# A transposed read in two halves, and one gate product in each bundle of a fused convolution and channel mix

## The chip, the cores and the metric

The kernel runs on one core of a Trainium2 chip. The metric is the device time of one execution in microseconds; three runs of the kernel before took 412.99, 415.35 and 415.41, with a median of 415.35.

## The reference

Input x is 8 batches of 4160 tokens of 192 channels. The first part is a causal convolution along the tokens with 7 taps; the taps of each of the 8 heads (24 channels each) are the softmax of its row of weights. The second part is a channel mix on its output y:

```python
y_prev = shift(y)                        # one token back, zero at the start
xk = mu_k * y + (1 - mu_k) * y_prev      # = y_prev + mu_k * (y - y_prev)
xr = mu_r * y + (1 - mu_r) * y_prev
k  = relu(xk @ w_k) ** 2                 # 192 -> 1024
v  = k @ w_v                             # 1024 -> 192
out = sigmoid(xr @ w_r) * v              # 192 -> 192
```

## The kernel before

Batches are worked on in four pairs. The channel mix needs y with channels on the partitions (yT: 64 channels of each of the two batches), cut into **steps** of 512 tokens of both batches (step 4 is tokens 1792 to 2304 of the first pair, step 5 the 512 after it). A step has 8 K products of 1024 columns (ps_k), a relu of each on ScalarE (k_sb, L605), a square on VectorE (k, L619), and V in two **quads** of 256 tokens (ps_v, L681). VectorE also forms d = y - y_prev (`diff`, L536), then xk and xr by scaling d with mu and adding y (L567, L573). R is `r` (L642 to L657, ps_r), its sigmoid `r_out` (L661), and `v_out` (L694) multiplies V by it and stores the output through SyncE (L705). Products, convolutions and R all take PSUM buffers from one ring of four (L56).

The order of all instructions is written out by hand. Four K products make a **bundle**, about 6 us long; there are 65, numbered from 0. `bundle_rest` (L930) gives one bundle's order: squares and VectorE's mixing work, K products 0 to 2, one R (the first in the table `rq` for this bundle), the first half of a quad's V, K product 3, any further R, the convolution units due in this bundle, and the second half of V. Tables give what falls due in a bundle: `mix_a`, `mix_b`, `mix_c` are run at three places among the squares, `late` at the end; `rq` and `rs` hold R and its sigmoid. SyncE's instructions are transfers alone, and they are issued in the order of the program, each with its waits.

The convolution works on **groups** of tokens of a pair. The first groups of the first pair are convolved on TensorE straight into the transposed layout. Every later group is convolved with tokens on the partitions, cast by ScalarE into a tile y (L337; two buffers), written to a buffer in memory by SyncE (`y_write`, L458), and read back transposed into yT by a DMA (`y_read`, L484). Group 4 (tokens 1920 to 3040 of the first pair) is the first of this kind. Its writes are put in `late` of bundle 3, its read in `mix_c` of bundle 4; groups 5, 6 and 7 are dense too and have a read of their own each. From group 8 on the units are "sparse" (`conv_sparse`, L350): each takes two ring buffers and fills two y tiles, and those groups are already read in two halves. The units of group 8 fall in bundles 14 to 17, those of group 9 in bundles 22 to 25.

In a dense group, y holds blocks of 56 tokens: 64 partitions hold one row of blocks, the other 64 another, and `y_write` needs four transfers (i: first or second half of the tokens, j: which 64 partitions).

xk and xr have two buffers each. With two, the R of step s must be done before step s + 2 is mixed, so line L808 caps R's bundle. This cap matters only after the first pair's last step, which is half as long: bundle 14 has two R's, bundle 17 has none.

Of the kernel before, what the change touches and what calls it, by code (L numbers as in the profile page):

```python
# [8 lines left out]
BF16 = mybir.dt.bfloat16  # L9
# [5 lines left out]
def kernel(  # L15
# [17 lines left out]
    P = 128  # L33
    NF = DF // P
    Q = 64
    NC = D // Q
# [8 lines left out]
    STEP = 512  # L45
# [7 lines left out]
    two = ctx.enter_context(tc.tile_pool(name="two", bufs=2))  # L53
    three = ctx.enter_context(tc.tile_pool(name="three", bufs=3))
# [19 lines left out]
    T0, LAST = S - TAIL, len(steps) - 1  # L74
# [11 lines left out]
    first_bundle = [bundle_of[st[3]] for st in steps]  # L86
# [365 lines left out]
    def new_yT(p):  # L452
        yTs[p] = two.tile([P, 3, -(-(YC + S) // 16) * 16], BF16, tag="yT", name="yT")
        y_drams[p] = dram.tile([NROW, 2 * D], BF16, tag=f"y{p % 2}", name="y_dram")
        nc.vector.memset(yTs[p][:, :, 0:YC], 0.0)


    def y_write(g):  # L458
        p, base, nb, _, _ = groups[g]
        if base == 0:  # L460
            new_yT(p)
        if g in sparse:
            m = nb // 4
            for half in range(2):
                for j in range(4):
                    nc.sync.dma_start(
                        out=bass.AP(
                            tensor=y_drams[p].tensor,
                            offset=y_drams[p].offset + (base + (2 * half * nb + j) * TB) * 2 * D,
                            ap=[[2 * D, TB], [4 * TB * 2 * D, 2 * m], [1, 2 * D]],  # L470
                        ),
                        in_=ys[g][half][32 * j : 32 * j + TB, :, :],
                    )
            return
        m = nb // 2
        for j in range(2):
            for i in range(2):
                r0 = base + (i * nb + j * m) * HB
                nc.sync.dma_start(  # L479
                    out=y_drams[p][r0 : r0 + m * HB, :].rearrange("(n t) c -> t n c", t=HB),  # L480
                    in_=ys[g][j * Q : j * Q + HB, i * m : (i + 1) * m, :],
                )
# [33 lines left out]
    diffs, xks, xrs = {}, {}, {}  # L516
# [23 lines left out]
    def mix(s, i, sl=slice(0, NC)):  # L540

        L = steps[s][2]
        d = diffs[s]
        if s == 0 and i == 0:
            if sl.start == 0:
                xks[s] = two.tile([P, NC, STEP], BF16, tag="xk", name="xk")
            t = xks[s]
            c = sl.start
            nc.vector.scalar_tensor_tensor(
                out=t[:, c, :L],  # L550
                in0=d[:, c, :L],
                scalar=mu[:, i, c : c + 1],
                in1=y_of(s, sl, 0)[:, 0, :],
                op0=ALU.mult,
                op1=ALU.add,
            )
            return
        scale(s, i, *range(sl.start, sl.stop))
        add_y(s, i, sl)

    def scale(s, i, *cs):
        L = steps[s][2]
        if s not in (xks, xrs)[i]:
            (xks, xrs)[i][s] = two.tile([P, NC, STEP], BF16, tag=("xk", "xr")[i], name=("xk", "xr")[i])
        t = (xks, xrs)[i][s]
        for c in cs:
            nc.vector.tensor_scalar(  # L567
                out=t[:, c, :L], in0=diffs[s][:, c, :L], scalar1=mu[:, i, c : c + 1], scalar2=None, op0=ALU.mult
            )
# [163 lines left out]
    early, rq, rs, xt, mix_a, mix_b, mix_c, vq, late = ({} for _ in range(9))  # L733

    def at(table, b, fn, *a):
        table.setdefault(b, []).append((fn, a))
# [7 lines left out]
    for g, (p, base, nb, fb, on_pe) in enumerate(groups):  # L744
        if g < 3:
            continue
        if p == 0:
            xs = {3: [1, 1], 4: [2, 2, 3, 3], 5: [4, 4, 5, 5]}[g]
        elif g not in sparse:
            xs = [fb - 9] * 2 + [fb - 7] * 2  # L750
        else:
            xs = {8: [14, 15, 16, 17], 9: [22, 23, 24, 25]}.get(g, [fb - 13, fb - 11, fb - 9, fb - 7])
        for i, b in enumerate(xs):
            xt.setdefault(b, []).append((g, i))
        if not on_pe:
            at(late, xs[-1], y_write, g)
        if g in sparse:
            at(late, max(fb - 5, xs[-1] + 2), y_read, g, slice(0, 1), 2)
            at(late, fb - 2, y_read, g, slice(1, 2), 2)
            b, b1 = {8: (9, 12), 9: (17, 18), 10: (24, 25)}.get(g, (fb - 19, fb - 16))  # L760
            at(early, b, x_tile, g)
            at(early, b, load_x, g, (0,))
            b = b1
            at(early, b, tie_x, g, 1)
            at(early, b, load_x, g, (1,))
            continue
        if not on_pe:
            at(mix_c if g == 4 else late, xs[-1] + (1 if g < 6 else 2), y_read, g)
        if g > 4:

            b = {5: 1, 6: 3, 7: 7}.get(g)
            b = first_bundle[first_step[p]] + (-15, -11, -7, -3)[(g - 6) % 4] if b is None else b
            table = {5: mix_a, 7: mix_c}.get(g, early)
            at(table, b, x_tile, g)
            at(table, b, load_x, g)
    for s, (p, t0, L, n0, ns) in enumerate(steps):
        fb = first_bundle[s]
        if s == 0:
            at(mix_a, 1, mix, s, 1)
            continue  # L780
        if s == 1:
            at(mix_b, 1, scale, s, 1, 0, 1)
            at(late, 2, scale, s, 1, 2)
            at(late, 2, add_y, s, 1)
        else:
            if s == 2:
                at(mix_c, 1, diff, s)
            elif s == 4:
                at(mix_b, fb - 1, diff, s)
            else:  # L790
                at(mix_c, fb - 2, diff, s)
            at(mix_b if s == 4 else mix_a, fb - 1, scale, s, 0, 0)
            at(mix_b, fb - 1, scale, s, 0, 1, 2)
            at(mix_c, fb - 1, add_y, s, 0)
            if s == 2:
                at(mix_a, fb, scale, s, 1, 0)
                at(mix_b, fb, scale, s, 1, 1)
            else:
                at(mix_c, fb - 1, scale, s, 1, 0)
                at(mix_a, fb, scale, s, 1, 1)  # L800
            at(mix_b, fb, scale, s, 1, 2)
            at(mix_b, fb, add_y, s, 1)
        if s == LAST - 1 or s < LAST and steps[s + 1][0] > p:
            at(late, fb - 1, keep_tail, p)
    for s, j, vb in quads:
        b = vb - (s == LAST)
        if 0 < s < LAST - 1:
            b = min(b, first_bundle[s + 2] - 2 + j)  # L808
        at(rq, b, r, s, j)
        at(rs, b, r_out, s, j)  # L810
        if s == LAST:
            at(late, vb, v_last, s, j)
        else:
            vq.setdefault(vb, []).append((s, j))
# [249 lines left out]
```

## Time and profile before

| | |
|---|---|
| runs, us | 412.99, 415.35, 415.41 |
| profiled execution, us | 412.98 |
| its span, us | 411.3 |
| TensorE busy (PE) | 401.3 us, 98% |
| VectorE busy (DVE) | 371.1 us, 90% |
| ScalarE busy (ACT) | 354.6 us, 86% |
| granted clock of TensorE | 0.999 |
| transposed reads of y (L488) | 14 |
| idle of d (L536) for such a read | 0.8 us, once |

Times within the profile count from the start of the span. PE is TensorE's matmuls and PEld its weight loads, SPq is SyncE's queue of transfers. The name of a group of instructions gives line, operation, output and inputs; an arrow "<-" behind an idle time names what released the instruction. An entry of SPq covers the issue of a transfer, not its movement.

### The profile page before, as it was taken

The numbers are of one execution on the slowest core, as the hardware profiler recorded it, in microseconds if no ns is written. First come the engines' busy times: TensorE is split into PE (matmuls) and PEld (weight loads), VectorE is DVE, ScalarE is ACT, GpSimd is POOL, SyncE is SP. The second block draws the span as 40 slices with busy tenths as digits, with TensorE's granted clock in tenths as the row PEclk, the third lists the DMA queues.
The fourth block names the chain that finished last, engine by engine and source line by source line (L and its number), as shares of the span: only waits on it lengthen the run. The fifth ranks groups of instructions, "written<-read, shape, count | busy, mean of one in ns | idle before, by whom it ended". The sixth has DMA issues, their size and how long they took to land.

```text
span 411.3 us, 17419 instructions
## 1 busy us (share of the span) xinstructions
PE 401.3 (98%) x7670; PEld 302.5 (74%) x7670; DVE 371.1 (90%) x672; ACT 354.6 (86%) x426; POOL 57.8 (14%) x91
## 2 busy tenths in 40 slices
PE   7899999999999999999999999999999999999996
PEld 4667767777777777777777777777777778777795
DVE  5899799999899998989999999999999899999973
ACT  6799978889998889988898998889898878877781
POOL 8623023030042002204020022100000001000000
PEclk9999999999999999999999999999999999999999
DMA  8999989997769988989995997979523756221223
GB/s 141 191 202 187 196 202 181 247 187 172 161 105 229 238 181 143 218 228 165 174 190 148 215 186 140 173 178 194 141 78 86 199 145 158 79 73 46 80 78 116
DMA packets 139091, 66.35 MB, mean 161 GB/s; under 512 B 89332, under 2 KB 139016, under 8 KB 139016
## 3 DMA queue, kind: packets, MB, share of 16 engines
q1 hardware_dynamic: 95672, 48.32, 48.3%
q0 software_dynamic: 42544, 16.36, 34.5%
q8 instruction: 60, 0.98, 1.0%
q10 hardware_dynamic: 800, 0.57, 0.5%
q14 instruction: 15, 0.12, 0.1%
HBM read 33.29 MB, written 36.99 MB: 171 GB/s over the span
## 4 chain that ended last, share of the span: by engine, by line
PE 87%; DMA 4%; DVE 4%; ACT 2%; POOL 1%; issue 1%; SPq 0%; POOLq 0%; ACTq 0%
PE ps_v L681 39%; PE ps_k L593 37%; PE ps_r L650 7%; PE ps_c L364 2%; DMA yT<-y_dram 2%; DMA wk<-in_moe_w_k_dram 2%; DVE k L619 2%; PE ps_v L633 1%; ACT k_sb L605 1%; DMA y_dram<-y 1%; PE ps_c L319 1%; ACT y L337 0%; DVE d L536 0%; POOL xb L154 0%; SPq L479 0%
## 5 line engine op out<-in xcount | busy, mean ns | idle before, releaser
L605 ACT ACTIVATE k_sb<-ps_k 128x1024 bf16<-128x1024 f32 x260 | 253.3, 1040 | 35.9 <-PE ps_k L593 35.2
L619 DVE TENSOR_TENSOR k<-k_sb 128x1024 bf16<-128x1024 bf16 x260 | 173.8, 689 | 26.0 <-ACT k_sb L605 25.9
L593 PE MATMUL ps_k<-xk,wk 64*128 64x512 bf16 (+1 forms) x1632 | 191.6, 367 | 2.0 <-DMA wk<-in_moe_w_k_dram 1.6
L681 PE MATMUL ps_v<-wv,k 64*128 64x192 bf16 x4032 | 188.6, 243 | 0.2 <-DVE k L619 0.2
L681 PEld LDWEIGHTS <-k 64*128 64x128 bf16 x4032 | 168.4, 94 | 13.2 <-issue 4.8
L593 PEld LDWEIGHTS <-wk 64*128 64x128 bf16 x1632 | 83.8, 94 | 57.2 <-DMA wk<-in_moe_w_k_dram 1.8
L154 POOL DMA_DIRECT2D xb<-in_x_dram x62 | 44.1, 720 | 142.8 <-DVE xb L125 58.7
L697 DVE TENSOR_TENSOR o_sb<-ps_v,r_sb 128x768 f32<-128x768 f32 x64 | 60.9, 951 | 3.3 <-issue 2.4
L661 ACT ACTIVATE r_sb<-ps_r 128x768 bf16<-128x768 f32 x65 | 53.6, 826 | 8.7 <-PE ps_v L681 7.0
L337 ACT CAST y<-ps_c 128x960 bf16<-128x960 f32 (+2 forms) x84 | 52.8, 709 | 0.2 <-DMA y_dram<-y 0.2
L650 PEld LDWEIGHTS <-xr 64*128 64x128 bf16 x780 | 34.8, 94 | 14.9 <-issue 1.0
L650 PE MATMUL ps_r<-wr,xr 64*128 64x192 bf16 x780 | 43.2, 243 | 0.5 <-DVE o_sb L697 0.5
L567 DVE TENSOR_SCALAR xr<-d,mu 128x512 bf16<-128x512 bf16 (+1 forms) x102 | 35.6, 353 | 0.0
L536 DVE TENSOR_TENSOR d<-yT 128x1536 bf16<-128x1536 bf16 (+4 forms) x36 | 31.2, 867 | 1.9 <-ACT yT L423 1.0
L567 DVE TENSOR_SCALAR xk<-d,mu 128x512 bf16<-128x512 bf16 (+1 forms) x99 | 32.1, 354 | 0.1
L573 DVE TENSOR_TENSOR xr<-xr,yT 128x1536 bf16<-128x1536 bf16 (+1 forms) x33 | 31.1, 942 | 1.1
L573 DVE TENSOR_TENSOR xk<-xk,yT 128x1536 bf16<-128x1536 bf16 (+3 forms) x33 | 30.6, 927 | 0.1
L520 POOL COPY y_tail<-yT 128x195 bf16<-128x195 bf16 x4 | 3.0, 762 | 89.3 <-DMA yT<-y_dram 89.3
L364 PEld LDWEIGHTS <-toe 32*32 32x32 bf16 x640 | 4.3, 87 | 8.9 <-issue 7.7
L364 PE MATMUL ps_c<-xb,toe 32*32 32x240 bf16 x640 | 9.4, 267 | 0.4 <-ACT k_sb L605 0.4
L127 POOL MEMSET xb<- 32x384 bf16 x3 | 1.2, 408 | 56.1 <-DVE xb L125 49.8
L413 PEld LDWEIGHTS <-xb 128*32 128x32 bf16 (+3 forms) x264 | 4.4, 104 | 2.5 <-ACT xb L247 1.1
(58 smaller groups left out, 65.0 us busy)
## 6 DMA issues: line engine op xcount, KB each, us to landing
out_dram<-o_sb SPq DMA_DIRECT2D x128, 192.0 KB
xb<-in_x_dram POOLq DMA_DIRECT2D x52, 240.0 KB, 8.5
y_dram<-y SPq DMA_DIRECT2D x40, 195.0 KB
y_dram<-y SPq DMA_DIRECT2D x16, 210.0 KB
xb<-in_x_dram POOLq DMA_DIRECT2D x4, 228.0 KB, 4.6
xb<-in_x_dram POOLq DMA_DIRECT2D x4, 192.0 KB, 6.6
wk<-in_moe_w_k_dram POOLq DMA_DIRECT2D x4, 192.0 KB, 7.4
xb<-in_x_dram POOLq DMA_DIRECT2D x2, 216.0 KB, 4.7
```

The lines of the kernel that those rows point to most:

```text
L154: nc.gpsimd.dma_start(out=xb[q0 : q0 + rows, lo:hi, s, :], in_=bass.AP(tensor=x.tensor, offset=x.offset + (b * S + t0 + lo * step) * D, ap ...
L337: nc.scalar.copy(out=bass.AP(tensor=y.tensor, offset=y.offset + d, ap=[y.ap[0], [m * 2 * D, 2], [2 * D, m], [Q, 2], [1, b - a]],), in_=bas ...
L536: nc.vector.tensor_tensor(out=shaped(s, diffs[s][:, cs, :L]), in0=y_of(s, cs, 1), in1=y_of(s, cs, 0), op=ALU.subtract)
L567: nc.vector.tensor_scalar(out=t[:, c, :L], in0=diffs[s][:, c, :L], scalar1=mu[:, i, c : c + 1], scalar2=None, op0=ALU.mult)
L573: nc.vector.tensor_tensor(out=o, in0=o, in1=y_of(s, sl, 0), op=ALU.add)
L593: nc.tensor.matmul(out=ps[:, i, f * L : (f + 1) * L], lhsT=wk[r, c, fs], rhs=xk[r, c, :L], start=c == 0 and f == 0, stop=c == NC - 1 and f ...
L605: nc.scalar.activation(out=k_sb, in_=ps.rearrange("p a b -> p (a b)"), func=AF.Relu)
L619: nc.vector.tensor_tensor(out=o, in0=i, in1=i, op=ALU.mult)
L650: nc.tensor.matmul(out=ps[:, i, k * D : (k + 1) * D], lhsT=xr[q, c, ts], rhs=wr[q, c, :], start=c == 0, stop=c == NC - 1,)
L661: nc.scalar.activation(out=r_sbs[s, j], in_=r_ps.pop((s, j))[:, :, 0 : 2 * D], func=AF.Sigmoid)
L681: nc.tensor.matmul(out=v_ps[s, j][:, bank, k * D : (k + 1) * D], lhsT=k2s[s][q, f, t * P : (t + 1) * P], rhs=wv[q, f, :], start=half == 0 ...
L697: nc.vector.tensor_tensor(out=o_sb.rearrange("p (b t) d -> p b (t d)", b=2), in0=v_ps.pop((s, j)), in1=r_sbs.pop((s, j)), op=ALU.mult,)
```

## The change

There are three edits.

1. `y_write`'s loop over token halves becomes the outer one, so the two transfers of the first 560 tokens of a group of 1120 are issued first. This holds for all four dense groups.
2. Group 4's transposed read becomes two: its first 560 tokens in `mix_c` of bundle 4, the second 560 in `late` of bundle 4. The reads of groups 5 to 7 stay whole and where they were.
3. xr gets three buffers, and the cap on R's bundle goes. R is then in the bundle of its own V quad: one R in each of bundles 14 to 17, where there were 2, 1, 1 and 0. No other bundle's R moves.

```diff
         m = nb // 2
-        for j in range(2):
-            for i in range(2):
+        for i in range(2):
+            for j in range(2):
                 r0 = base + (i * nb + j * m) * HB
                 nc.sync.dma_start(
...
         if s not in (xks, xrs)[i]:
-            (xks, xrs)[i][s] = two.tile([P, NC, STEP], BF16, tag=("xk", "xr")[i], name=("xk", "xr")[i])
+            (xks, xrs)[i][s] = (two, three)[i].tile([P, NC, STEP], BF16, tag=("xk", "xr")[i], name=("xk", "xr")[i])
...
         if not on_pe:
-            at(mix_c if g == 4 else late, xs[-1] + (1 if g < 6 else 2), y_read, g)
+            if g == 4:
+                at(mix_c, 4, y_read, g, slice(0, 1), 2)
+                at(late, 4, y_read, g, slice(1, 2), 2)
+            else:
+                at(late, xs[-1] + (1 if g < 6 else 2), y_read, g)
...
     for s, j, vb in quads:
         b = vb - (s == LAST)
-        if 0 < s < LAST - 1:
-            b = min(b, first_bundle[s + 2] - 2 + j)
         at(rq, b, r, s, j)
         at(rs, b, r_out, s, j)
```

## The prediction

> **What bounds the kernel now.** I read the busy totals, then who waited for whom, then the chain that ended last around each wait of TensorE, then the stages.
>
> ```profile
> PE 401.3 (98%) x7670; PEld 302.5 (74%) x7670; DVE 371.1 (90%) x672; ACT 354.6 (86%) x426; POOL 57.8 (14%) x91
> ```
>
> TensorE is idle for 411.3 - 401.3 = 10.0 us, most of it in the first 20 us. So nothing that leaves its work alone can bring much: the question is which stalls after 20 us the two edits touch. The list of waits has two of them, each with the wait that stands behind it:
>
> ```profile
> DVE d L536 <- DMA yT<-y_dram: 0.8, 1, 0.8
> PE ps_r L650 <- DVE o_sb L697: 0.5, 1, 0.5
> PE ps_c L364 <- ACT k_sb L605: 0.4, 1, 0.4
> ACT y L337 <- DMA y_dram<-y: 0.2, 1, 0.2
> ```
>
> The chain, in order of time (start, length), ties the first two together: y's write, the transposed read, d, then VectorE's queue up to o_sb, whose PSUM buffer R's product then takes.
>
> ```profile
> 38.16 4.37 DMA y_dram<-y
> 42.68 7.31 DMA yT<-y_dram
> 50.01 0.98 DVE d L536
> 55.70 0.88 DVE o_sb L697
> 56.62 0.67 PE ps_r L650 x12
> ```
>
> SyncE's queue in the same stretch (start, length of the issue):
>
> ```profile
> 39.51 2.02 SPq L705 DMA_DIRECT2D out_dram<-o_sb  x2
> 42.68 3.93 SPq L488 DMA_TRANSPOSE yT<-y_dram  x1
> 46.72 1.82 SPq L705 DMA_DIRECT2D out_dram<-o_sb  x2
> ```
>
> I measure a bundle from the start of its predecessor's second run of 32 V matmuls to the start of its own. In the stages (from:to, length, then busy PE, PEld, DVE, ACT, POOL, clock, DMA share, GB/s) these are bundles 5 and 7, then 14 to 17, then 24:
>
> ```profile
> 40.36:46.72 6.36, 6.36 (x121) 4.58 (x118) 5.61 (x10) 6.26 (x9) 0.00 (x0) 1.00 0.73 181
> 52.46:59.73 7.27, 6.70 (x120) 4.54 (x116) 7.24 (x14) 5.34 (x7) 0.38 (x1) 1.00 0.74 192
> ...
> 96.05:103.40 7.35, 6.95 (x150) 5.04 (x146) 6.41 (x13) 7.25 (x10) 0.00 (x0) 1.00 0.50 137
> 103.40:109.61 6.21, 6.21 (x166) 5.58 (x158) 5.44 (x13) 5.83 (x8) 0.00 (x0) 1.00 0.80 149
> 109.61:116.08 6.47, 6.47 (x150) 4.58 (x134) 6.16 (x10) 6.47 (x10) 0.00 (x0) 1.00 0.62 157
> 116.08:121.77 5.69, 5.69 (x130) 3.95 (x122) 4.88 (x10) 5.40 (x9) 4.29 (x7) 1.00 0.52 73
> ...
> 157.29:163.61 6.32, 6.32 (x142) 4.60 (x134) 6.08 (x11) 6.32 (x10) 2.74 (x4) 1.00 0.79 96
> ```
>
> Bundles 5 and 7 hold the same work (one R, two dense convolution units): 7 is 7.27 - 6.36 = 0.91 us too long. Bundle 24 (one R, one sparse unit) has ScalarE busy for all of 6.32 us: where such bundles follow one another, ScalarE is the bound. Bundles 14 to 17 have one sparse unit each and 2, 1, 1, 0 R's; together they last 7.35 + 6.21 + 6.47 + 5.69 = 25.72 us.
>
> **What the Trainium skill says.** "Perfetto Trace Analysis", section "DMA Instruction — HWDGE (DVE, Sync)": such an instruction's span ends when its descriptors are generated, and the movement is not in it. The trace agrees: the read's issue took 3.93 us, the chain counts 7.31 until it landed, so 3.38 us come after the issue. "DMA: Bandwidth & Descriptors", "Two DMAs through the same engine are not ordered": a DMA that reads what another wrote needs the writer's completion semaphore, the common queue doesn't do. Hence the read stands behind its writes, and only a write order by halves lets half a read start early; the trace has SyncE's read at 42.68, just after the last write landed at 38.16 + 4.37 = 42.53. Same page, "DMA Transpose (X-bar)": the partition count must be a multiple of 16; 560 rows are, and both halves are one stream from SyncE. No run shows a half read yet.
>
> **The change, part by part.**
>
> *Writes by halves.* The same four writes, all released by the same ScalarE cast, so groups 5 to 7 change nothing. For group 4 the first two issues now hold the first 560 rows. Cost 0.
>
> *The half read.* It needs the first two writes, and its issue follows the two output stores that end at 39.51 + 2.02 = 41.53. Issue from 41.6 at the earliest, from 42.6 at the latest (the last write's landing). Its length isn't in the trace: at best half of 3.93 = 1.97 (estimate from the whole read's), at worst the whole 3.93. With 3.38 after it, it lands between 41.6 + 1.97 + 3.38 = 46.9 and 42.6 + 3.93 + 3.38 = 49.9. VectorE was ready for d at 50.01 - 0.80 = 49.21. I take 47: the wait goes, 2 us to spare. Step 4 (tokens 1792 to 2304) needs rows of group 4 up to 2304, and the first half reaches 1920 + 560 = 2480.
>
> VectorE then has d, xk and o_sb 0.80 us earlier, R finds its buffer, and bundle 7 shrinks to bundle 5's length: **-0.9 us**. Bounds: 0 (lands at 49.9) and -0.9; what is late next is nothing within 0.9, since bundles 8 to 13 alternate between 5.7 and 6.4 us (without and with units) and no wait of theirs is in the list.
>
> *The second half read.* One more issue on SyncE. Behind it stand the output stores of 46.72, then group 5's writes. If each half took 3.3 us to issue (what the whole read after this one took), SyncE would be free at 41.6 + 6.6 = 48.2, not 46.6; group 5's writes go from 49.12 to about 50, and its read lands about 1 us later, some 8 us before its first reader. The second half lands by 51.6; its reader, d of step 5, runs at 58.95. Output buffers are three deep. Cost 0; with that cover gone it would be up to 1.6.
>
> *The third R buffer.* 3 KB per partition and no instruction. It takes from VectorE the wait of xr's first scale on an earlier R. No xr wait is in the list, and xr's group shows no idle time: 0.
>
> *One R in each bundle.* One R (12 matmuls, 0.49 us) and its sigmoid (0.83 us on ScalarE) leave bundle 14; every later R moves on by a bundle and bundle 17 gets one. Sum of work 0. TensorE's stall of 0.40 in bundle 14 goes: there the second conv tile took the buffer that a relu freed late. At best the four bundles become one of 6.20 and three of 6.32, that is 25.16: -0.56. But ScalarE is the slower engine here, and its casts in bundle 14 are held by something else:
>
> ```profile
> 103.59 0.97 ACT L337 CAST y<-ps_c 128x960 bf16<-128x960 f32 x1
> 104.72 0.96 ACT L337 CAST y<-ps_c 128x960 bf16<-128x960 f32 x1 [0.16 <-DMA y_dram<-y]
> ```
>
> The second cast writes the y buffer that group 7's write must have left, and that landed at 104.7. Without the second sigmoid the first cast comes at 102.9 and the second is ready at 103.8, yet starts at 104.72 all the same: the wait grows from 0.16 to 0.95 and eats the gain. From there ScalarE has bundle 15's relus at 105.58 as before; it saves its idle 0.22 (bundle 15) and 0.29 (bundle 17), but bundle 17 has 0.83 more to do: 0.83 - 0.51 = 0.3 us later at the end of bundle 17. TensorE feels part of it. In bundle 17 ScalarE starts 0.22 earlier, at 118.09, does three relus (2.72) and the sigmoid (0.81), and at 121.62 frees the buffer for the second conv tile; V's second run follows 0.33 later at 121.95, against 121.77. **+0.2 us**; bounds -0.56 and +0.3.
>
> **Sum.** -0.9 + 0.2 = -0.7. The profiled execution took 412.98 (span 411.3 and 1.7 around it), so 412.3. The runs shown are 412.99, 415.35 and 415.41: one agrees with the profile, two are 2.4 us longer for a reason that this trace doesn't hold. I predict on the profiled level and keep the other as a case.
>
> **The rivals.**
>
> 1. *Both edits pay*: group 7's write lands a microsecond sooner and the cast doesn't wait: 412.98 - 0.9 - 0.56 = 411.5. For it: the 0.40 stall. Against it: the cast's wait exists already.
> 2. *The longer level stays*: 415.35 - 0.7 = 414.65. For it: two of three runs. Against it: if the 2.4 us are a late transposed read, the half read removes them.
> 3. *The edit doesn't do what it says*: the half lands no earlier than the whole did, and only the 0.2 counts: 413.2. For it: a transposed read's issue ran from 3.2 to 7.5 us for nearly equal sizes, so size isn't all.
> 4. *Slower*: the half read starts in the midst of the remaining writes and stores and issues as slowly as the slowest read, 7.52 us. It lands at 41.6 + 7.52 + 3.38 = 52.5, VectorE waits 3.3 us, not 0.8, at d of step 4, and bundle 7 grows by 2.5: 412.98 + 2.5 + 0.2 = 415.7. It decides from a landing after 50.0. Against it: those writes end by 43, and input loads don't run in this stretch.
>
> **How the numbers follow.** Forecast (412.3) 45%, both pay 14%, longer level 25%, nothing gained 9%, slower 7%. The range 411.3 to 415.2 holds the first four with their bounds and leaves out rival 4 and tails. A change of under 1% is about what a measurement of this kernel can't tell from none: 411.2 to 419.5. Below it only the lower tail of rival 1 and an unexpected extra, 7%; above it only rival 4 on the longer level (418.1) with something more, 4%; within, 89%.
>
> **What would show it.** d of step 4 without a wait on yT; R in bundle 7 without a wait on o_sb; bundle 7 at about 6.4 us. In bundle 14 no stall of ps_c on a relu, but a cast's wait on y_dram near 0.9 us; bundles 14 to 17 together 25.5 to 26.0 us. Two transposed issues of about 2 us each in place of 3.93. I am wrong if the half lands after 49.2, if the cast's wait doesn't grow, or if the level of the runs moves for a reason outside both places.

## The result and the profile after

The changed kernel takes 413.03 us (median of 22 runs, 411.26 to 413.99), the kernel before 414.37 us (22 runs, 412.94 to 415.95). The ratio is 0.9966, with a 95% interval of 0.9953 to 0.9979: faster by 0.9 to 1.9 us, about 1.4. That is within 1%, as forecast, and twice the 0.7 us of the sum. The profiled execution took 412.6 us with a span of 410.9.

The list of waits of the kernel after has no wait of d (L536) on yT any more, nor one of R on o_sb. Where the change acts, these two have come instead:

```profile
ACT y L337 <- ACT y L337: 0.4, 1, 0.4
PE ps_k L593 <- ACT y L337: 0.2, 1, 0.2
```

SyncE's queue and VectorE around group 4's read, from the timeline of the kernel after (start, length):

```profile
39.77 2.26 SPq L705 DMA_DIRECT2D out_dram<-o_sb  x2
42.89 4.00 SPq L488 DMA_TRANSPOSE yT<-y_dram  x2
46.94 1.76 SPq L705 DMA_DIRECT2D out_dram<-o_sb  x2
...
49.86 0.96 DVE L536 TENSOR_TENSOR d<-yT 128x1536 bf16<-128x1536 bf16 x1
```

Two issues take 4.00 us, where one took 3.93. d follows o_sb directly. The stages of the kernel after, cut as before: bundle 7, then 14 to 17, then 21.

```profile
53.19:59.57 6.38, 6.38 (x120) 4.59 (x116) 6.34 (x12) 5.35 (x7) 0.39 (x1) 1.00 0.71 172
95.89:102.11 6.22, 6.22 (x138) 4.46 (x134) 5.28 (x11) 6.12 (x9) 0.00 (x0) 1.00 0.42 120
102.11:108.88 6.77, 6.59 (x166) 5.80 (x158) 6.65 (x15) 6.40 (x8) 0.00 (x0) 1.00 0.96 190
108.88:115.13 6.25, 6.25 (x141) 4.53 (x134) 6.07 (x10) 6.18 (x10) 0.00 (x0) 1.00 0.65 132
115.13:121.53 6.40, 6.40 (x142) 4.53 (x134) 5.35 (x12) 6.40 (x10) 4.35 (x7) 1.00 0.62 87
138.72:144.46 5.74, 5.74 (x103) 4.48 (x101) 5.74 (x11) 4.58 (x6) 0.00 (x0) 1.00 1.11 260
```

Bundle 7 fell from 7.27 to 6.38 us. Bundles 14 to 17 sum to 25.64, against 25.72: bundle 14 is short now, and bundles 15 and 17 are longer. Their casts, in ScalarE's timeline:

```profile
102.75 0.95 ACT L337 CAST y<-ps_c 128x960 bf16<-128x960 f32 x1
104.07 0.96 ACT L337 CAST y<-ps_c 128x960 bf16<-128x960 f32 x1 [0.37 <-ACT y L337]
```

The second cast waits 0.37 us, not 0.16. The profile names the cast before it, which had ended by then; R's move alone, below, has a wait in the same place that is put down to the write.

The spans differ by only 0.4 us because the start differed the other way: bundle 3 ended at 34.72 after and at 33.98 before. That is scatter: up to there the order of work is the same in both, and over all profiles it ends between 33.2 and 34.7.

### The profile page after: what moved, and what is told of

Read it like the earlier page. It is cut to its first block, busy times and chain, and to the rows that moved or that the text cites. A ratio compares the mean times of both kernels' runs of the same rounds, so it can differ in the third digit from the quotient of the medians.

```text
span 410.9 us, 17418 instructions
## 1 busy us (share of the span) xinstructions
PE 402.1 (98%) x7669; PEld 302.7 (74%) x7670; DVE 371.5 (90%) x672; ACT 354.6 (86%) x426; POOL 57.9 (14%) x91
## 4 chain that ended last, share of the span: by engine, by line
PE 91%; DMA 3%; DVE 2%; ACT 2%; issue 1%; SPq 0%; POOL 0%; ACTq 0%; POOLq 0%
PE ps_v L681 40%; PE ps_k L593 39%; PE ps_r L650 8%; PE ps_c L364 2%; DMA xb<-in_x_dram 2%; PE ps_v L633 1%; DMA y_dram<-y 1%; PE ps_c L319 1%; ACT k_sb L605 1%; ACT y L337 1%; PE ps_t L413 1%; DVE k L619 1%; SPq L479 0%; DVE d L536 0%; DVE xr L567 0%
## 5 line engine op out<-in xcount | busy, mean ns | idle before, releaser
L650 PEld LDWEIGHTS <-xr 64*128 64x128 bf16 x780 | 34.7, 94 | 14.2
L536 DVE TENSOR_TENSOR d<-yT 128x1536 bf16<-128x1536 bf16 (+4 forms) x36 | 31.2, 867 | 2.4 <-ACT yT L423 2.4
L413 PE MATMUL ps_t<-toe,xb 128*32 128x120 bf16 (+3 forms) x264 | 6.7, 272 | 0.8 <-DMA xb<-in_x_dram 0.5
```

The lines of the kernel that those rows point to most:

```text
L536: nc.vector.tensor_tensor(out=shaped(s, diffs[s][:, cs, :L]), in0=y_of(s, cs, 1), in1=y_of(s, cs, 0), op=ALU.subtract)
L650: nc.tensor.matmul(out=ps[:, i, k * D : (k + 1) * D], lhsT=xr[q, c, ts], rhs=wr[q, c, :], start=c == 0, stop=c == NC - 1,)
```

## The experiments

Each run has its median and then its ratio to the kernel before in the same set of runs, with a 95% interval. The ratio is not the quotient of two medians: in the first three runs the median before was 414.57, and for the very first that quotient would be 0.9963. Edits are against the kernel before unless said otherwise. "Bundles 14 to 17" is the sum of the four.

### The half read alone

The first two edits (writes by halves, half read); xr and the cap on R as before.

```diff
-        for j in range(2):
-            for i in range(2):
+        for i in range(2):
+            for j in range(2):
...
-            at(mix_c if g == 4 else late, xs[-1] + (1 if g < 6 else 2), y_read, g)
+            if g == 4:
+                at(mix_c, 4, y_read, g, slice(0, 1), 2)
+                at(late, 4, y_read, g, slice(1, 2), 2)
+            else:
+                at(late, xs[-1] + (1 if g < 6 else 2), y_read, g)
```

> Writes by halves and group 4's read in two halves; R and its buffers as before. Theory (the half read is the whole gain, R's move is worth nothing because the cast's wait on group 7's write takes its place): bundle 7 about 6.4 us, bundles 14 to 17 together 25.7 us as before, total 0.9 us under before, ratio about 0.998. Rival (R's move pays as well): only about half of the full change's gain, ratio 0.9985 or above.

413.05 us, ratio 0.9973 (0.9958 to 0.9988). Bundle 7 is 6.38 us, bundles 14 to 17 sum to 25.71. The stages are as the theory had them. The ratio is a little below its figure, and its interval holds both readings. It stands for a gain of 1.1 us; bundle 7 accounts for 0.8 to 0.9 of it, and this profile doesn't show the rest.

### R's move alone

```diff
-            (xks, xrs)[i][s] = two.tile([P, NC, STEP], BF16, tag=("xk", "xr")[i], name=("xk", "xr")[i])
+            (xks, xrs)[i][s] = (two, three)[i].tile([P, NC, STEP], BF16, tag=("xk", "xr")[i], name=("xk", "xr")[i])
...
-        if 0 < s < LAST - 1:
-            b = min(b, first_bundle[s + 2] - 2 + j)
```

> Third buffer for xr and one R in each bundle; group 4's read whole, writes in the old order. Theory: bundle 7 at 7.3 us, bundles 14 to 17 together 25.5 to 25.9 us, ratio 1.000. Rival (R's move pays): bundles 14 to 17 together 25.2 us or less, ratio 0.9988.

414.16 us, ratio 0.9985 (0.9970 to 1.0000). Bundle 7 is 7.38 us. Bundles 14 to 17 sum to 25.95: R's move *costs* 0.2 us there. ScalarE's timeline of this kernel:

```profile
105.13 0.96 ACT L337 CAST y<-ps_c 128x960 bf16<-128x960 f32 x1 [0.69 <-DMA y_dram<-y]
```

Here the wait has its name, group 7's write, and has grown from 0.16 to 0.69. Yet the ratio leans under 1, though its interval reaches 1.0000: something outside these bundles may gain.

### The half read with the old write order

Only the second edit: the lines on `y_read` of the diff above, with the loop over j still the outer one.

> Group 4's read in two halves, its four writes in the old order, so the first half waits for the first and the third write; R as before. Theory of the half's size (what brings it in time is that it is half as long, the four writes land together anyway): the first issue starts within 0.4 us of where it starts with the new write order, bundle 7 about 6.4 us, ratio 0.998. Rival (the write order is what lets it start early): the first half is late for d, bundle 7 above 6.8 us, ratio 0.999 to 1.0.

413.75 us, ratio 0.9969 (0.9946 to 0.9993). SyncE's read and the stage of bundle 7:

```profile
41.53 3.98 SPq L488 DMA_TRANSPOSE yT<-y_dram  x2
```

```profile
51.70:58.08 6.38, 6.38 (x120) 4.59 (x118) 6.35 (x12) 5.35 (x7) 0.40 (x1) 1.00 0.81 208
```

The read starts 1.9 us after the end of bundle 4, against 1.8 in the changed kernel, and bundle 7 is as short. For bundle 7 the write order isn't needed; what counts is that the first read brings half. Whether it changes the start, one pair of profiles doesn't tell; more of them stand below, under the half's start.

### The halves swapped

Against the changed kernel, the half that step 4 needs comes second:

```diff
-                at(mix_c, 4, y_read, g, slice(0, 1), 2)
-                at(late, 4, y_read, g, slice(1, 2), 2)
+                at(mix_c, 4, y_read, g, slice(1, 2), 2)
+                at(late, 4, y_read, g, slice(0, 1), 2)
```

> The changed kernel with the two half reads issued in the other order: the half that step 4 needs comes second. Theory (the gain is that the needed half lands before VectorE reaches d, by about 2 us; two half reads as such bring nothing): the needed half lands where a whole read did, d waits 0.3 to 0.9 us, bundle 7 is 6.7 to 7.3 us instead of 6.38, ratio to before 0.998 to 1.0. Rival (two short reads are faster than one long one, whatever their order): no wait, bundle 7 at 6.4 us.

413.7 us, ratio 0.9988 (0.9973 to 1.0004). SyncE's reads, VectorE's timeline, then bundle 7:

```profile
42.99 4.86 SPq L488 DMA_TRANSPOSE yT<-y_dram  x2
```

```profile
49.89 0.96 DVE L536 TENSOR_TENSOR d<-yT 128x1536 bf16<-128x1536 bf16 x1 [0.68 <-DMA yT<-y_dram]
```

```profile
52.38:59.52 7.14, 6.67 (x120) 4.53 (x114) 7.11 (x13) 5.34 (x7) 0.31 (x1) 1.00 0.68 170
```

The wait is back, and with it 0.76 us of bundle 7. Two half reads as such bring nothing here; the needed half has to be the first.

The swap changes one thing more: the half that now comes first needs the last two writes, so it starts 2.6 us after the end of bundle 4, not 1.8, and the needed half is late for that reason too. The trace tells the two apart. A whole read of group 4 moves 3360 packets of 256 bytes, a half 1680. Here the first 1680 had been moved by 47.9, and d, which follows a read's last packet by 0.5 us in the six profiles where it waits, was ready at 49.2. So a half that starts as late as a whole read is still in time, if it is the first.

### Group 7 earlier, with and without R's move

What makes the cast wait would be taken away most directly by a third buffer for y. It does not fit: with it 4.375 KB of memory per partition were left where another pool of buffers needs 8. Instead, group 7's last two units and its write move from bundle 13 to 12; its read stays in bundle 15. The first run has this on the changed kernel, the second the same with R capped and two xr buffers.

```diff
+        elif g == 7:
+            xs = [11, 11, 12, 12]
         elif g not in sparse:
             xs = [fb - 9] * 2 + [fb - 7] * 2
...
-                at(late, xs[-1] + (1 if g < 6 else 2), y_read, g)
+                at(late, {7: 15}.get(g, xs[-1] + (1 if g < 6 else 2)), y_read, g)
```

> The changed kernel with the last two convolution units of group 7, and its write, one bundle earlier (bundle 12 instead of 13), so that the write has left its y buffer before group 8's second cast; its read stays in bundle 15. Theory (the cast's wait eats R's gain): no wait of a cast on y_dram in bundle 14, bundle 15 at 6.2 to 6.3 us instead of 6.77, bundles 14 to 17 together 24.9 to 25.2 us instead of 25.63, ratio to before 0.9952 to 0.9958. Rival (ScalarE's work bounds these bundles): 25.5 us or more, ratio as the changed kernel, 0.9966.

> Half reads and group 7 earlier as in the run on group 7, but xr with two buffers and R capped as before (2, 1, 1, 0 in bundles 14 to 17). Theory (with the cast's wait gone R's move would pay): the stall on a relu stays in bundle 14, which is 7.1 to 7.3 us; bundles 14 to 17 together 25.4 to 25.7 us, 0.4 to 0.6 us over the run with R moved. Rival (an earlier write alone repairs these bundles): the same sum as with R moved, within 0.1 us.

With R moved: 412.44 us, ratio 0.9954 (0.9935 to 0.9973). With R capped: 413.6 us, ratio 0.9985 (0.9970 to 1.0001). Bundles 14 to 17 with R moved:

```profile
94.59:100.77 6.18, 6.18 (x134) 4.46 (x130) 5.07 (x11) 5.17 (x7) 0.00 (x0) 1.00 0.63 202
100.77:107.11 6.34, 6.34 (x172) 5.68 (x156) 6.30 (x14) 6.33 (x8) 0.00 (x0) 1.00 0.56 88
107.11:113.45 6.34, 6.34 (x144) 4.58 (x132) 6.30 (x11) 6.34 (x10) 0.00 (x0) 1.00 0.63 161
113.45:119.76 6.31, 6.31 (x145) 4.60 (x132) 5.43 (x12) 6.30 (x10) 4.33 (x7) 1.00 0.57 74
```

They sum to 25.17, ScalarE busy throughout in the last three; no cast waits for y_dram. With R capped they sum to 25.71, and bundle 14 is 7.34 with the old stall of 0.40 on a relu. So R's move is worth 0.54 us once the cast's wait is gone, which is what the prediction gave as its best case. The edit also frees bundle 13 of casts, so the wait isn't isolated; but with R capped the same edit gains nothing in these bundles.

### A store's wait in bundle 21

Profiles of several kernels differ most at one more place, bundle 21. The kernel before was profiled twice more, the changed one once more.

> The kernel before once more, to see how its stalls scatter between executions. If the late read is the same in all executions, bundle 7 is 7.2 to 7.4 us again; if it scatters, it lies anywhere from 6.4 to 9 us, and the gain of the half read is larger than one profile shows. The place where runs differ by 2 us is the first 25 us or a store's wait in bundle 21 or later.

> The same as the run before it: a third profile of the kernel before, with the same two readings.

> The changed kernel once more: bundle 7 at 6.37 us, since the needed half lands some 2 us before it is wanted; the cast's wait in bundle 14 anywhere from 0.3 to 0.95 us and bundles 14 to 17 together 25.6 to 26.0 us.

The kernel before: bundle 7 at 6.89 and 7.25 us (7.27 in the first profile), bundle 21 at 6.76 and 7.18 us (5.79 in the first). The changed one: bundle 7 at 6.37, bundles 14 to 17 at 25.70, bundle 21 at 5.78. So the late read of group 4 does scatter, by 0.4 us in bundle 7, and the place in bundle 21 by 1.4. Waits of the third profile of the kernel before, around bundle 21, and the chain there:

```profile
DVE o_sb L697 <- DMA out_dram<-o_sb: 1.4, 1, 1.4
PE ps_r L650 <- DVE o_sb L697: 1.3, 1, 1.3
```

```profile
131.84 10.86 DMA out_dram<-o_sb
142.82 0.97 DVE o_sb L697
143.83 0.67 PE ps_r L650 x12
```

A store took 10.86 us to land, and VectorE waited for its buffer, one of three. In all profiles with R capped and three output buffers bundle 21 took 5.79, 6.76, 7.18, 5.74, 6.77 and 7.07 us; with R moved 5.74, 5.78, 6.13, 5.73 and 6.21. A fourth output buffer, in both places where o_sb is made, takes this wait away:

```diff
-        o_sb = three.tile([P, 4, D], FP32, tag="o_sb", name="o_sb")
+        o_sb = four.tile([P, 4, D], FP32, tag="o_sb", name="o_sb")
```

> The kernel before with a fourth output buffer, which takes the wait for a store out of bundle 21 (0.06, 1.0 and 1.4 us over its 5.73 us in three profiles of the kernel before). Theory of the hidden part (R's move gains in bundle 21, since the input loads of bundle 17 start 0.5 us earlier against the writes after them, and not in bundles 14 to 17): bundle 21 at 5.73 us, bundle 7 at 7 us, ratio 0.998. Rival (the stores are not in the runs' time): ratio 1.000.

> The changed kernel with a fourth output buffer. Theory of the hidden part: its bundle 21 lost next to nothing (5.74 and 5.78 us in two profiles), so the fourth buffer brings it under 0.3 us, ratio 0.996 to 0.9966, and the distance to the kernel before with four output buffers is 0.7 to 0.9 us, which is bundle 7 alone (ratio of the two 0.998). Rival: it gains as much as the kernel before does, ratio 0.9945.

On the kernel before: 413.5 us, ratio 0.9981 (0.9966 to 0.9996), bundle 21 at 5.74 us. On the changed one: 412.64 us, ratio 0.9960 (0.9944 to 0.9976), bundle 21 at 5.74 us. Bundle 21 in the third profile of the kernel before, then with the fourth buffer:

```profile
139.33:146.51 7.18, 5.90 (x106) 4.47 (x102) 5.83 (x11) 4.58 (x6) 0.00 (x0) 1.00 1.12 157
139.52:145.26 5.74, 5.74 (x104) 4.48 (x102) 5.74 (x11) 4.59 (x6) 0.00 (x0) 1.00 1.13 236
```

The kernel before gains about 0.8 us by it, the changed one 0.2 (0.9966 to 0.9960, inside the intervals), and the two are then 0.86 us apart in medians, which is bundle 7 (7.22 and 6.37 us in their profiles). This points to the store's wait as the part of the gain that the sum didn't have; the intervals don't prove it.

With R moved the wait was under 0.5 us in all five profiles, with R capped it was over 1 us in four of six. Why it should be rarer with R's move is not shown. The two timelines fit one reading: bundle 17 is now the longer one, and the loads of x that start with it lead the following writes of y by more. These are GpSimd's loads and SyncE's writes, first of before, then of after:

```profile
117.70 2.77 POOL L154 DMA_DIRECT2D xb<-in_x_dram  x4
```

```profile
123.42 7.05 SPq L466 DMA_DIRECT2D y_dram<-y  x8
```

```profile
116.70 2.90 POOL L154 DMA_DIRECT2D xb<-in_x_dram  x4
```

```profile
122.97 7.12 SPq L466 DMA_DIRECT2D y_dram<-y  x8
```

The lead is 5.7 us before and 6.3 us after, so stores may meet less of the loads. But it is 5.7 in all six profiles with R capped, and two of them lost next to nothing in bundle 21, so the lead alone doesn't decide it. A rival is the transposed read that SyncE issues among these stores: it took 7.5 to 8.7 us to issue with R capped and 5.9 to 7.7 with R moved, and where bundle 21 lost over 1 us it took at least 7.58 (though 7.63 in a profile that lost nothing). Which of the two is the cause isn't known; no run moved the loads or that read alone.

### Both remedies together

Group 7 earlier and the fourth output buffer, on the changed kernel.

> The run on group 7 with a fourth buffer for the output tile. In two profiles bundle 21 lost 0.4 to 1.0 us because an output store behind a slow transposed read held its buffer; with a fourth one no o_sb waits for a store, bundle 21 is 5.73 us in every profile, and the runs scatter less at the upper end: ratio to before 0.994 to 0.9955. If stores are not part of the scatter between runs, the ratio is that of the run on group 7.

412.35 us over 8 runs (411.26 to 413.38), ratio 0.9946 (0.9923 to 0.9969). Bundle 21 was 5.74 us and no o_sb waited for a store. It is the lowest ratio of all, but its interval overlaps that of the run on group 7 alone, so the fourth buffer's part on top of it stays unproven. It beats the kernel before; its lead over the changed one is 0.2%, with overlapping intervals.

## Why the prediction was right, and where its sum was off

**The half read: right.** -0.9 us at bundle 7, and 7.27 became 6.38. The cause is shown by the swapped halves (0.68 us of wait and 7.14 us again) and by the half read alone. Three profiles of the kernel before have 7.27, 6.89 and 7.25: on average the step is worth 0.76. The second half cost nothing, as the prediction had it: group 5's writes start 8.8 us after the end of bundle 4 before and after.

**The half's start: earlier, as predicted, but the gain doesn't rest on it.** I let the first half start early because its two writes come first. It started 0.4 to 2.0 us after the end of bundle 4 in the seven profiles with that order (1.8 in the first), a whole read 2.3 to 2.8 us after it in five. So the order does bring the start forward. In the one profile with the old order the half started at 1.9, and bundle 7 was as short: in it and in the changed kernel the first half's packets are all moved about 2.6 us before d would have had to wait for them. The prediction had 2 to spare. What failed is only "only a write order by halves lets half a read start early", as a condition of the gain.

**"Writes by halves. Cost 0": wrong by a little, for group 7.** SyncE issues its four writes sooner in the new order. The first line is R's move alone (old order), the second the changed kernel:

```profile
99.03 3.06 SPq L479 DMA_DIRECT2D y_dram<-y  x4
```

```profile
98.28 2.42 SPq L479 DMA_DIRECT2D y_dram<-y  x4
```

In both they start 2.4 us after the end of bundle 13. The second cast starts 8.5 us after it with the old order and 8.2 with the new: the write leaves the y buffer 0.3 us sooner. This fits the wait that takes the stall's place: 0.31 to 0.43 in the four profiles with R moved and the new order, 0.69 in the one with the old.

**R's move: mechanism right, size off.** The step said that the cast's wait grows from 0.16 to 0.95 and that bundles 14 to 17 lose 0.2. Alone the move does that: 0.69 of wait, +0.23. With the new write order it is 0.37 of wait and -0.08, 0.3 better than the term of the sum.

**What the sum didn't have: bundle 21, and more scatter.** The profile of before had only 0.06 us of loss in bundle 21, and I took that one execution for the kernel. Two others lost 1.0 and 1.4 us to a store. Over the profiles (three of before, two of after) bundle 7 gives 7.14 - 6.38 = 0.76, bundles 14 to 17 give 0.05, and bundle 21 gives 6.58 - 5.76 = 0.82, together 1.6 us. Against it stand 0.33 in bundle 31 and 0.21 in bundle 38, where the second profile of the changed kernel is longer; that leaves 1.1 apart from the start, and the medians have 1.3. Bundle 38 took 5.77 us in the four profiles of the kernel before with three or four output buffers, and 6.05 to 6.70 in nine of the ten of the other kernels. In seven of these nine TensorE waits there at R, 0.2 to 0.8 us, for nothing that the profile shows; the cause is open. The share of each part is open too. These profiles give bundle 21 as much as the half read. The ratios of the runs lean to the half read: with it and R as before they stand for 1.1, 1.3 and, with group 7 earlier, 0.6 us, with R moved and d still waiting for 0.6 and 0.5. The intervals hold either reading.

**How much was luck.** The forecast was 412.3 and the median is 413.03, but two errors met there. The level of 412.98 that I started from was 1.4 us under the median of the kernel before, and the change was 0.6 us too small. Its direction and the gain at bundle 7 were not luck. Two readings were also wrong, without weight in the sum: TensorE's idle time lies not mostly in the first 20 us (4.5 of 10.0; another 4.1 are in the last 11), and 22 runs of each kernel tell apart far less than 1%.

**The rivals.** "Both pay" was right that R's move could give 0.54, and wrong in this kernel, where the cast's wait stands in front of it. "The longer level" isn't one: with 22 runs the kernel before spreads evenly from 412.9 to 416.0 and the changed one from 411.3 to 414.0. The start (bundle 3 ends at 33.2 to 34.7 us over all profiles), bundle 21 and the bundles just named are sources of that spread. The slower rival (a half read that issues slowly and lands after 50) appeared in no profile.

## What to carry to other kernels

When a stall on one buffer goes, look at what else the same engine waits for within the next microsecond: here a cast's wait on a write took most of the stall's place, and only moving that write, with the casts before it, freed the gain. If a transfer is late by less than its length, read first the part that is needed first. One profile shows one execution: a wait of 0.06 us in it can be over 1 us in the next, so waits on long transfers should be looked at in several.

## What was not expected of the hardware

The same four writes of 56 x 5 rows took SyncE 2.4 us to issue for group 7 when they alternate between the two partition halves (2.40 to 2.42 in the five profiles with this order and group 7 in its old place) and 3.04 to 3.06 us when two of the same half follow one another (six profiles). For groups 4 to 6 the difference is less clean (2.4 to 3.2 against 2.9 to 3.2). The order of the places in memory changes along with that of the partitions; which of them counts, and why, was not tried.

Two half reads of group 4 took 3.6 to 4.9 us to issue together in nine profiles, and the whole read 3.5 to 5.2 in five: halving this read added no issue time on SyncE that stands out from the scatter.
